# An attention and max-out kernel: attention in four runs of matmuls per group, loads, decoding and weight splits placed anew

## The chip, the cores and the metric

The kernel runs on one NeuronCore of a Trainium2 chip. The metric is the device time of one execution in microseconds (us), lower is better. The engines are TensorE (PE: matmuls; its weight loads are a row of their own, PEld), VectorE (DVE), ScalarE (ACT), GpSimd (POOL) and SyncE (SP, which issues nearly all DMAs).

## The reference

Attention with a sigmoid instead of a softmax feeds a layer that takes the largest of three products, and one more product.

```python
scores = scale * q @ k.T - log(S)          # batch 8, 12 heads, S = 448, head width 64
attn_out = sigmoid(scores) @ v
x = attn_out.transpose(0, 2, 1, 3).reshape(8 * 448, 12 * 64)     # 3584 x 768
h = maximum(maximum(x @ w1, x @ w2), x @ w3)                     # each weight 768 x 768
out = h @ w_out
```

## The kernel before

**Attention.** Heads are taken in pairs (one qk tile holds q and k of two heads, 64 partitions each) and two pairs make a group, so there are 24 groups, the loop over `n` at L394. Keys come in three chunks of 128 and a remainder of 64. `scores` (L325) multiplies one chunk for both heads of a pair side by side, in three fp32r terms made of high and low parts (`qk_split`, L317, on VectorE), and ends in one sigmoid of 2 x 448 columns on ScalarE. `last_scores` (L336) does the remainders of both pairs in plain F32, `weigh` (L348) multiplies a chunk's sigmoids by v in F32, `last_weigh` (L355) does so for the remainder. An F32 matmul stands in the trace as two records. A group's order on TensorE is: the first pair's scores, the second pair's weighing of the group before and its `last_weigh`, `last_scores`, the second pair's scores, the first pair's weighing. Scores go through three tiles `ps_s` of two PSUM banks each, weighing through two banks `ps_av`. `finish` (L373) copies these out on VectorE and stores them to `x_dram`.

Beside this, weights are decoded from 64-bit floats in blocks (`decoding`, L156; two steps on ScalarE, four on VectorE), combined on GpSimd (`w_combine`) and split into high and low parts (`w_split`, L151). From group 9 on, x blocks are loaded back and combined on GpSimd (`x_combine`).

Before the first group, 12 matmuls on zeros run (L388). TensorE's clock has two levels, 1.2 and 2.4 GHz.

**Layers.** Four stages (three weights and the output weight) times four pairs of batches make 16 visits (`n` at L507). A visit has three passes `q`, each of seven products of 2x2 blocks (`PRODUCTS`, L28) with nine fp32r matmuls of 448 columns (`product`, L446), so 16 x 3 x 7 x 9 = 3024 matmuls. A place is written (n, q, k). Before a product's operand can be used, ScalarE casts its high part (`x_hi`, L257) and VectorE subtracts (`x_lo`, L263). Tables fix the places: `his` and `los` for x, `ws` for weight splits, `w_loads` for weight loads and combinations, `decodes` for decoding. `put` (L515) adds a product's bank to what it needs on VectorE and, where a block is done, stores it. The turn into the last stage is at visit 12.

Everything runs in the order of the program on each engine (`pin`), SP's queue included: a load that waits for its buffer holds back what stands behind it.

Of the kernel before, what the change touches and what calls it, by code (L numbers as in the profile page):

```python
# [17 lines left out]
P = 128  # L18
D = 64
# [3 lines left out]

# [12 lines left out]
def attention_then_maxout(  # L40
# [8 lines left out]

# [29 lines left out]
    xs_p = pool(ctx, "xs", 1)  # L100
# [3 lines left out]


# [20 lines left out]


# [28 lines left out]
    def decoding(dec_p, todo, bufs, ahead, square_p):  # L156
# [35 lines left out]
        for k, (st, q, n) in enumerate(todo):  # L192
            while len(raws) < min(k + ahead, len(todo)):
                raws.append(load(*todo[len(raws)]))
            if k == 0:
                yield
# [13 lines left out]

    def x_block(r, src, p, row, th, k=None):

        name = f"b{row + 1}{th + 1}"
        if name not in r:
            r[name] = xs_p.tile([P, HALF, S], F32, name=f"xs_{name}")
        ks = slice(0, HALF) if k is None else slice(k, k + 1)
        t = (2 * p + th) * S
        pin(nc.sync.dma_start(out=r[name][:, ks], in_=src[row][:, ks, t : t + S]))

    def x_combine(r, names=TOKENS, ks=range(HALF)):  # L220

        for name in names:
            if name not in r:
                r[name] = (
                    r["b12"] if name == "t3" else xs_p.tile([P, HALF, S], F32, name=f"xs_{name}")
                )
# [13 lines left out]
    def t_store(r, p):  # L240
        for k, name in enumerate(TOKENS):
            pin(nc.sync.dma_start(out=t_dram[p][:, k], in_=r[name]))

    def x_load_all(p):
        r = {}
        for _, name, _ in PRODUCTS:
            if name in TOKENS:
                tile_name = "xs_b12" if name == "t3" else f"xs_{name}"
                r[name] = xs_p.tile([P, HALF, S], F32, name=tile_name)
# [18 lines left out]
    def attention(stack):  # L268

        dec_p = pool(stack, "dec", 2)
        sq_p = pool(stack, "sq", 2)
# [3 lines left out]
        a_p = pool(stack, "a", 8)  # L277
# [5 lines left out]
        background = decoding(dec_p, todo, 2, 3, sq_p)  # L283
        splits = []

# [10 lines left out]
        def load_qk(b, k):  # L296
            t = qk_p.tile([P, 2 * S], F32, name="qk")
            if b == k == 0:
# [11 lines left out]
        def sigmoid(ps):  # L310
            a = a_p.tile([P, 2, S], F32, name="a")
            pin(nc.scalar.activation(  # L312
                out=a, in_=ps[:, :, :S], func=AF.Sigmoid, bias=bias_s, scale=scale
            ))
            return a
# [9 lines left out]
        def scores(terms, c):  # L325
            ps = ps_s.tile([P, 2, 512], F32, name="ps_s")
            for n, (kt, qt) in enumerate(terms):
                for e in range(2):
                    r = slice(e * D, (e + 1) * D)
                    pin(nc.tensor.matmul(  # L330
                        ps[:, e, :S], kt[r, S + c * P : S + (c + 1) * P], qt[r, :S],
                        start=n == 0, stop=n == len(terms) - 1,
                    ))
            return sigmoid(ps)

        def last_scores(ts):  # L336
# [9 lines left out]
            return sigmoid(ps)  # L346

        def weigh(ps, vt, g, c, a):  # L348
            for e in range(2):
                pin(nc.tensor.matmul(  # L350
                    ps[e * D : (e + 1) * D, :S], vt[:, (g * C + c) * 2 + e], a[:, e],
                    start=c == 0, stop=False,
                ))

        def last_weigh(pss, vt, a):  # L355
            for g, ps in enumerate(pss):
                r = slice(g * D, (g + 1) * D)
                for e in range(2):
                    pin(nc.tensor.matmul(
                        ps[e * D : (e + 1) * D, :S], vt[r, 4 * C + e], a[r, e],  # L360
                        start=False, stop=True,
# [5 lines left out]
        def load(n):  # L367
            if n < len(fours):
                b, f = fours[n]
                ts = load_qk(b, 2 * f), load_qk(b, 2 * f + 1)  # L370
                loads[n] = ts, load_v(b, f)

        def finish(n, pss, pool=m_p, names=("m11", "m12")):  # L373
            b, f = fours[n]
            for g, ps in enumerate(pss):
# [7 lines left out]
        load(0)  # L383

# [3 lines left out]
        for n in range(12):  # L388
# [4 lines left out]
        terms = [(loads[0][0][0],) * 2]  # L393
        for n in range(len(fours) + 1):  # L394
            if n < len(fours):
                load(n + 1)
                ts, vt = loads.pop(n)
                first = [scores(terms, c) for c in range(C)]
                terms = qk_split(ts[1])
                if n == 0:  # L400
                    decode()
                for _ in range(2):
                    if splits:
                        w_split(*splits.pop(0), nc.vector.tensor_copy)
# [3 lines left out]
            if before:  # L408
                pvt, pss, second, last = before
                for c in range(C):  # L410
                    weigh(pss[1], pvt, 1, c, second[c])
                last_weigh(pss, pvt, last)
                if n == len(fours):
                    break
# [208 lines left out]
```

## Time and profile before

| | us |
|---|---|
| median of three runs | 884.75 |
| lowest, highest | 883.69, 893.62 |
| span of the profiled execution | 882.5 |
| TensorE busy in the span | 874.1 |

The span reaches from the first to the last instruction of the profiled execution; the run's time also holds what lies around it. TensorE's busy time counts from a matmul's start to its modelled end, and matmuls overlap, so the steps between starts tell more than the share. "x12" merges twelve records of one kind; "[1.21 <-DMA qk<-qk]" is idle time ahead of a group and what ended it. In the windows, the columns are the stretch, its length, and for PE, PEld, DVE, ACT and POOL the busy time with the number of instructions, then the granted clock, the DMA engines' busy share and GB/s.

### The profile page before, as it was taken

To read this page: it belongs to the slowest core of one execution; us is meant where nothing else is said; L and a number is where in the kernel's file an instruction comes from. 1 tells how busy PE (TensorE), PEld (TensorE's weight loads), DVE (VectorE), ACT (ScalarE), POOL (GpSimd) and SP (SyncE) were. 2 spreads that over 40 slices of the span, in tenths; PEclk is the share of its full clock that TensorE was granted. 3 is DMA by queue.
4 is the path that set the end of the run, shared out by engine and by line. 5 is a ranking of instruction groups with operands and counts; after the bars stand their busy time and mean duration, and the time that the engine had idled before them with its cause. 6 is when DMAs were issued, how large, how long until landed. Compare 5 with 4: busy or idle time off the path is not lost. (4 is left out here: it accounts for less than half of the span.)

```text
span 882.5 us, 12993 instructions
## 1 busy us (share of the span) xinstructions
PE 874.1 (99%) x4866; PEld 696.1 (79%) x4866; DVE 621.3 (70%) x875; ACT 392.9 (45%) x499; POOL 183.2 (21%) x148
## 2 busy tenths in 40 slices
PE   8999999999999999999999999999999999999998
PEld 4544455444459999999999999999999998899997
DVE  3677568766866948678696888878778596736442
ACT  5777767776672413342353343235334253423320
POOL 0100022023102563502100020210001543760600
PEclk9999999999999999999999999999999999999999
DMA  6667666786647455414745642484563426162412
GB/s 225 208 227 240 226 236 224 243 279 228 214 158 275 174 217 165 174 50 141 292 159 207 241 147 70 148 298 170 182 263 114 150 77 222 65 209 94 169 72 83
DMA packets 74350, 161.87 MB, mean 183 GB/s; under 512 B 6960, under 2 KB 53808, under 8 KB 74288
## 3 DMA queue, kind: packets, MB, share of 16 engines
q1 hardware_dynamic: 74208, 160.82, 52.0%
q8 instruction: 38, 0.62, 0.3%
q10 hardware_dynamic: 80, 0.23, 0.1%
q14 instruction: 24, 0.20, 0.1%
HBM read 109.90 MB, written 51.12 MB: 182 GB/s over the span
## 5 line engine op out<-in xcount | busy, mean ns | idle before, releaser
L312 ACT ACTIVATE a<-ps_s,bias_s 128x896 f32<-128x896 f32 x168 | 156.4, 1007 | 78.6 <-PE ps_s L342 59.4
L451 PE MATMUL ps_y<-xhi_t,wlo_s 128*128 128x448 f32 x432 | 158.1, 366 | 0.1
L451 PE MATMUL ps_y<-xhi_t,whi_s 128*128 128x448 f32 x432 | 158.0, 366 | 0.0
L451 PE MATMUL ps_y<-xlo_t,whi_s 128*128 128x448 f32 x432 | 157.9, 366 | 0.0
L350 PE MATMUL ps_av<-a,v 128*64 128x448 f32 x576 | 118.6, 548 | 0.0
L451 PE MATMUL ps_y<-xhi_b,wlo_a 128*128 128x448 f32 x288 | 105.4, 366 | 0.0
L451 PE MATMUL ps_y<-xlo_b,whi_a 128*128 128x448 f32 x288 | 105.3, 366 | 0.0
L451 PE MATMUL ps_y<-xhi_b,whi_a 128*128 128x448 f32 x288 | 105.3, 366 | 0.0
L141 POOL TENSOR_TENSOR ws_s<-ws_a,ws_a 128x384 f32<-128x384 f32 x12 | 14.3, 1194 | 412.9 <-DMA ws_a<-w_dram 315.8
L549 ACT COPY p<-ps_y 128x448 f32<-128x448 f32 x48 | 25.5, 531 | 156.4 <-PE ps_y L451 156.4
L451 PEld LDWEIGHTS ps_y<-xhi_t,wlo_s 128*128 128x128 f32 x432 | 81.3, 188 | 6.8 <-ACT xhi_b L260 0.5
L451 PEld LDWEIGHTS ps_y<-xhi_t,whi_s 128*128 128x128 f32 x432 | 81.3, 188 | 6.3
L451 PEld LDWEIGHTS ps_y<-xlo_t,whi_s 128*128 128x128 f32 x432 | 81.3, 188 | 6.2
L350 PEld LDWEIGHTS ps_av<-a,v 128*64 128x64 f32 x576 | 37.2, 136 | 59.4 <-issue 57.9
L523 DVE TENSOR_TENSOR m<-ps_y,u 128x448 f32<-128x448 f32 x72 | 44.7, 621 | 55.9 <-PE ps_y L451 55.9
L229 POOL TENSOR_TENSOR xs_t<-xs_b,xs_t 128x448 f32<-128x448 f32 x48 | 64.2, 1363 | 37.0 <-DMA xs_b<-x_dram 36.0
L264 DVE TENSOR_TENSOR xlo_t<-xs_t,xhi_t 128x1344 fp32r<-128x1344 f32 x42 | 68.4, 1628 | 3.0 <-ACT xhi_t L260 3.0
L521 ACT COPY m<-ps_y 128x448 f32<-128x448 f32 x24 | 12.8, 533 | 125.8 <-PE ps_y L451 122.2
L552 DVE TENSOR_TENSOR u<-ps_y,p 128x448 f32<-128x448 f32 x48 | 29.9, 622 | 53.6 <-PE ps_y L451 52.5
L264 DVE TENSOR_TENSOR xlo_b<-xs_b,xhi_b 128x1344 fp32r<-128x1344 f32 x42 | 66.5, 1584 | 0.0
L260 ACT CAST xhi_t<-xs_t 128x1344 fp32r<-128x1344 f32 x42 | 55.5, 1322 | 17.7 <-PE ps_y L451 9.0
L175 ACT ACTIVATE c<-wraw 128x384 f32<-128x384 f32 x48 | 27.0, 563 | 75.4 <-DVE m L529 44.9
(68 smaller groups left out, 1636.1 us busy)
## 6 DMA issues: line engine op xcount, KB each, us to landing
qk<-qk SPq DMA_DIRECT2D x47, 448.0 KB, 5.6
xs_b<-x_dram SPq DMA_DIRECT2D x30, 672.0 KB, 7.0
wraw<-w SPq DMA_DIRECT2D x36, 384.0 KB, 4.9
xs_t<-t_dram SPq DMA_DIRECT2D x18, 672.0 KB, 8.0
v<-v SPq DMA_DIRECT2D x24, 448.0 KB, 3.8
h_dram<-m SPq DMA_DIRECT2D x48, 224.0 KB, 1.9
xs_b<-h_dram SPq DMA_DIRECT2D x16, 672.0 KB, 6.5
outT<-m SPq DMA_DIRECT2D x48, 224.0 KB, 1.9
```

The source lines that it names most:

```text
L141: pin(nc.gpsimd.tensor_tensor(out=r[name], in0=r[in0], in1=r[in1], op=op))
L175: pin(nc.scalar.activation(out=square, in_=high.bitcast(F32), func=AF.Square))
L229: pin(nc.gpsimd.tensor_tensor(out=r[name][:, k], in0=r[in0][:, k], in1=r[in1][:, k], op=ALU.subtract))
L260: pin(nc.scalar.copy(out=hi, in_=r[name]))
L264: pin(nc.vector.tensor_tensor(out=lo, in0=x, in1=hi.bitcast(F32), op=ALU.subtract))
L312: pin(nc.scalar.activation(out=a, in_=ps[:, :, :S], func=AF.Sigmoid, bias=bias_s, scale=scale))
L350: pin(nc.tensor.matmul(ps[e * D : (e + 1) * D, :S], vt[:, (g * C + c) * 2 + e], a[:, e], start=c == 0, stop=False,))
L451: pin(nc.tensor.matmul(ps[:, :S], wt[:, k * P : (k + 1) * P], xt[:, k], start=first and n == 0, stop=n == len(terms) - 1, skip_group_check ...
L521: pin(nc.scalar.copy(out=m[name], in_=y))
L523: pin(nc.vector.tensor_tensor(out=m[name], in0=y, in1=add, op=ALU.add))
L549: pin(nc.scalar.copy(out=p1, in_=ps[0][:, :S]))
L552: pin(nc.vector.tensor_tensor(out=u2, in0=ps[1][:, :S], in1=p1, op=ALU.add))
```

## The change

Attention's order in a group becomes: `last_scores`, all six score chunks, then for the group before all six weighings and `last_weigh`. The third chunk of the first pair writes its scores to the `ps_av` banks as two tiles, with one sigmoid for each; the other chunks keep `ps_s`. In group 23 `last_weigh` comes before the weighings. qk tiles are loaded two groups ahead and v in its own group; the first two qk tiles come in halves over two queues. Both pairs' splits for the next group are made in the group before. The loads of raw weight blocks (`fetch`) and their decoding are separate steps, with fewer buffers; one block's decoding moves from attention to place (1, 0, 6), and the x operand t4 is combined and stored after attention. 18 matmuls run on zeros instead of 12. One matmul, at (0, 1, 0), takes 478 columns instead of 448. In the turn to the last stage the weight splits of the first set move from visit 11's second pass to its first, those of the second set from visit 12 partly to visit 11, the third set's from k = 4 to 6 to k = 2 to 4 of the second pass, and with them the weight loads; the x load of visit 12 moves from k = 6 to k = 4. The very last block is added and stored in two halves, the second one over ScalarE's queue.

```diff
-        sq_p = pool(stack, "sq", 2)
+        sq_p = pool(stack, "sq", 1)
-        a_p = pool(stack, "a", 8)
+        a_p = pool(stack, "a", 9)
...
-        background = decoding(dec_p, todo, 2, 3, sq_p)
+        todo.insert(19, todo.pop(15))
+        todo.pop()
+        background = decoding(dec_p, todo, 1, 2, sq_p)
...
-            if b == k == 0:
+            if b == 0 and k < 2:
                 pin(nc.scalar.dma_start(out=t[D:], in_=qk[b, k, D:]))
                 pin(nc.sync.dma_start(out=t[:D], in_=qk[b, k, :D]))
...
+        def sigmoid(banks, **kw):
+            a = a_p.tile([P, 2, S], F32, name="last" if kw else "a", **kw)
+            parts = (
+                [(a[:, e], ps[:, :S]) for e, ps in enumerate(banks)]
+                if type(banks) is list else [(a, banks[:, :, :S])]
+            )
+            for out, ps in parts:
+                pin(nc.scalar.activation(
+                    out=out, in_=ps, func=AF.Sigmoid, bias=bias_s, scale=scale
+                ))
             return a
...
+        def accumulators():
+            return [ps_av.tile([P, 512], F32, name=f"ps_av{g}") for g in range(2)]
...
+        def weigh(banks, vt, chunks, ahead):
+            for g, ps in enumerate(banks):
+                for c, a in enumerate(chunks[g]):
+                    for e in range(2):
+                        pin(nc.tensor.matmul(
+                            ps[e * D : (e + 1) * D, :S], vt[:, (g * C + c) * 2 + e], a[:, e],
+                            start=c == 0 and not ahead, stop=c == C - 1 and ahead,
+                        ))
...
         load(0)
+        load(1)
...
-        for n in range(12):
+        for n in range(18):
...
             if n < len(fours):
-                load(n + 1)
-                ts, vt = loads.pop(n)
-                first = [scores(terms, c) for c in range(C)]
-                terms = qk_split(ts[1])
+                ts = loads.pop(n)
+                if n != 1:
+                    fetch()
+                if n:
+                    last = last_scores(ts)
+                    load(n + 2)
+                    vt = load_v(*fours[n])
+                    for _ in range(2):
+                        if splits:
+                            w_split(*splits.pop(0), nc.vector.tensor_copy)
+                first = [scores(terms[0], c, accumulators() if c == C - 1 else None)
+                         for c in range(C)]
                 if n == 0:
+                    terms = None, qk_split(ts[1])
+                    last = last_scores(ts)
+                    vt = load_v(*fours[n])
+                    load(n + 2)
+                ahead = loads.get(n + 1)
+                after = [qk_split(ahead[0]) if ahead else None]
+                if n:
                     decode()
+                second = [scores(terms[1], c) for c in range(C)]
+                after.append(qk_split(ahead[1]) if ahead else None)
+                terms = after
...
-                x_combine(xs, ((), ("t1",), ("t2", "t3"), ("t4",))[block], (k,))
+                x_combine(xs, ((), ("t1",), ("t2", "t3"), ())[block], (k,))
...
+            if before:
+                pvt, chunks, rest = before
+                banks = accumulators()
+                if n == len(fours) - 1:
+                    last_weigh(banks, pvt, rest, True)
+                    weigh(banks, pvt, chunks, True)
+                else:
+                    weigh(banks, pvt, chunks, False)
+                    last_weigh(banks, pvt, rest, False)
+                if n < len(fours):
+                    finish(n - 1, banks)
+            before = vt, (first, second), last
...
+            moving, cols = xt[:, k], S
+            if wide and n == 0:
+                cols = S + 30
+                moving = xt[:].rearrange("p a s -> p (a s)")[:, :cols]
...
             else:
-                when = [[(n - 1, 1, 4 + k // 3) for k in range(7)],
-                        [(n, 0, 1)] * 2 + [(n, 0, 4)] * 2 + [(n, 0, 5)] * 2 + [(n, 0, 6)],
-                        [(n, 1, 4 + k // 3) for k in range(7)]]
+                when = [[(n - 1, 0, k) for k in (1, 1, 4, 4, 4, 5, 6)],
+                        [(n - 1, 2, 5)] + [(n - 1, 2, 6)] * 2 + [(n, 0, 4)] * 4,
+                        [(n, 1, 2 + k // 3) for k in range(7)]]
...
-    decodes = [
+    decodes = [(1, 0, 6)] + [
...
-    todo = [(st, q, n) for st in (2, 3) for q in range(3) for n in range(4)]
+    todo = [(1, 2, 3)] + [(st, q, n) for st in (2, 3) for q in range(3) for n in range(4)]
...
-    for _, name, _ in PRODUCTS[1:4]:
+    x_combine(xs, ("t4",))
+    for _, name, _ in PRODUCTS[1:5]:
         x_lo(*x_hi(name, xs))
...
+                    elif (n, q, name) == (done - 1, 2, "12"):
+                        row, t = q * P, (2 * p + 1) * S
+                        for r, dma in ((slice(0, S // 2), nc.sync), (slice(S // 2, S), nc.scalar)):
+                            pin(nc.vector.tensor_tensor(
+                                out=m[name][:, r], in0=y[:, r], in1=add[:, r], op=ALU.add
+                            ))
+                            pin(dma.dma_start(
+                                out=outT[row : row + P, t + r.start : t + r.stop],
+                                in_=m[name][:, r],
+                            ))
+                        return
...
-                product(ps[bank], w_ops[q][wname], x_ops[xname], first)
+                product(ps[bank], w_ops[q][wname], x_ops[xname], first, here == (0, 1, 0))
...
-                if here == (n, 0, 6 if (n, 0, 6) in w_loads else 4) and nst in (0, LAST):
+                if here == (n, 0, 4) and nst in (0, LAST):
                     xs = x_load(x_dram if nst == 0 else h_dram, np_)
```

## Rows read from the trace of the kernel before

**Rows 1.** The page, busy time, share of the span, instructions by engine

```profile
PE 874.1 (99%) x4866; PEld 696.1 (79%) x4866; DVE 621.3 (70%) x875; ACT 392.9 (45%) x499; POOL 183.2 (21%) x148
```

**Rows 2.** Timeline of TensorE (PE) at the start: start, duration, line, operation

```profile
1.05 2.93 PE L391 MATMUL ps_s<-idle 64*128 64x128 f32 x24 [1.05 <-DVE bias_s L87]
5.19 4.74 PE L330 MATMUL ps_s<-qk 64*128 64x448 f32 x12 [1.21 <-DMA qk<-qk]
9.86 0.98 PE L342 MATMUL ps_s<-qk 64*64 64x448 f32 x8
```

**Rows 3.** Timeline of VectorE (DVE), start and first groups

```profile
7.33 0.63 DVE L321 CAST hi<-qk 128x896 fp32r<-128x896 f32 x1 [6.33 <-DMA qk<-qk]
7.99 1.09 DVE L322 TENSOR_TENSOR lo<-qk,hi 128x896 fp32r<-128x896 f32 x1
...
20.65 1.16 DVE L378 COPY m<-ps_av 128x448 f32<-128x448 f32 x2 [2.29 <-PE ps_av L359]
```

**Rows 4.** Timeline of TensorE over one attention group

```profile
20.43 0.93 PE L342 MATMUL ps_s<-qk 64*64 64x448 f32 x8
21.30 0.47 PE L330 MATMUL ps_s<-hi 64*128 64x448 f32 x2
21.60 0.36 PE L330 MATMUL ps_s<-lo,hi 64*128 64x448 f32 x2
...
22.62 0.43 PE L330 MATMUL ps_s<-hi 64*128 64x448 f32 x2
22.89 0.37 PE L330 MATMUL ps_s<-lo,hi 64*128 64x448 f32 x2
23.09 0.37 PE L330 MATMUL ps_s<-hi,lo 64*128 64x448 f32 x2
23.39 2.48 PE L350 MATMUL ps_av<-a,v 128*64 128x448 f32 x12
25.80 0.47 PE L330 MATMUL ps_s<-hi 64*128 64x448 f32 x2
...
31.02 0.93 PE L342 MATMUL ps_s<-qk 64*64 64x448 f32 x8
```

**Rows 5.** Timeline of TensorE at the end of attention

```profile
256.30 4.73 PE L350 MATMUL ps_av<-a,v 128*64 128x448 f32 x24
260.96 0.98 PE L359 MATMUL ps_av<-a,v 64*64 64x448 f32 x8
261.87 0.47 PE L451 MATMUL ps_y<-xhi_b,wlo_a 128*128 128x448 f32 x1
```

**Rows 6.** Timeline of ScalarE (ACT) in the same group as rows 4

```profile
21.52 3.70 ACT L312 ACTIVATE a<-ps_s,bias_s 128x896 f32<-128x896 f32 x4 [2.60 <-PE ps_s L342]
25.09 0.58 ACT L175 ACTIVATE c<-wraw 128x384 f32<-128x384 f32 x1
```

**Rows 7.** Busy time of each engine in stretches of the layers

```profile
400.00:500.00 100.00, 100.00 (x495) 92.82 (x494) 79.35 (x120) 36.28 (x52) 8.11 (x8) 1.00 0.54 194
600.00:700.00 100.00, 100.00 (x495) 92.80 (x495) 77.16 (x104) 37.27 (x46) 9.89 (x9) 1.00 0.53 192
700.00:800.00 100.00, 97.65 (x477) 88.87 (x476) 71.23 (x85) 38.10 (x50) 52.83 (x40) 1.00 0.37 129
```

**Rows 8.** Waits of TensorE by line and releaser, total, times, longest

```profile
PE ps_y L451 <- DVE m L523: 2.1, 1, 2.1
```

**Rows 9.** Timeline of GpSimd (POOL) in the turn

```profile
747.25 4.45 POOL L229 TENSOR_TENSOR xs_t<-xs_b,xs_b 128x448 f32<-128x448 f32 x3 [3.48 <-DMA xs_b<-h_dram]
```

**Rows 10.** Timeline of VectorE in the turn

```profile
758.05 2.26 DVE L264 TENSOR_TENSOR xlo_t<-xs_t,xhi_t 128x1344 fp32r<-128x1344 f32 x1 [2.98 <-ACT xhi_t L260]
```

**Rows 11.** Last addition on VectorE, and stores by kind

```profile
878.78 0.62 DVE L523 TENSOR_TENSOR m<-ps_y,u 128x448 f32<-128x448 f32 x1 [1.21 <-PE ps_y L451]
...
outT<-m SPq DMA_DIRECT2D x48, 224.0 KB, 1.9
...
w_dram<-wb SPq DMA_DIRECT2D x36, 192.0 KB, 1.9
```

More of the change, by code (lines that the diff above doesn't have):

```diff
@@ L209, in attention_then_maxout, with xs_tile @@
     TOKENS = tuple(SUMS)
+    def xs_tile(name):
+        return xs_p[name == "t4"].tile([P, HALF, S], F32, name=f"xs_{name}")
     def x_block(r, src, p, row, th, k=None):
@@ L214, in x_block @@
         if name not in r:
-            r[name] = xs_p.tile([P, HALF, S], F32, name=f"xs_{name}")
+            r[name] = xs_tile(name)
         ks = slice(0, HALF) if k is None else slice(k, k + 1)
@@ L223, in x_combine @@
             if name not in r:
-                r[name] = (
-                    r["b12"] if name == "t3" else xs_p.tile([P, HALF, S], F32, name=f"xs_{name}")
-                )
+                r[name] = r["b12"] if name == "t3" else xs_tile(name)
             in0, in1 = SUMS[name]
@@ L323, in qk_split, with scores @@
             return (hi, hi), (hi, lo), (lo, hi)
-        def scores(terms, c):
-            ps = ps_s.tile([P, 2, 512], F32, name="ps_s")
+        def accumulators():
+            return [ps_av.tile([P, 512], F32, name=f"ps_av{g}") for g in range(2)]
+        def scores(terms, c, banks=None):
+            if banks is None:
+                banks = ps_s.tile([P, 2, 512], F32, name="ps_s")
+            bank = banks if type(banks) is list else [banks[:, e] for e in range(2)]
             for n, (kt, qt) in enumerate(terms):
@@ L345, in last_scores, with last_weigh @@
                     ))
[L346 to L356, printed above, removed]
+            return sigmoid(ps, bufs=2)
+        def weigh(banks, vt, chunks, ahead):
[6 more added lines that the diff above has]
+                        ))
+        def last_weigh(banks, vt, a, ahead):
+            for g, ps in enumerate(banks):
                 r = slice(g * D, (g + 1) * D)
@@ L360, in last_weigh @@
                         ps[e * D : (e + 1) * D, :S], vt[r, 4 * C + e], a[r, e],
-                        start=False, stop=True,
+                        start=ahead, stop=not ahead,
                     ))
@@ L407, in attention @@
                     x_lo(*x_hi(name, xs))
[L408 to L414, printed above, removed]
-                finish(n - 1, pss)
-            last = last_scores(ts)
-            second = [scores(terms, c) for c in range(C)]
-            if n + 1 < len(fours):
-                terms = qk_split(loads[n + 1][0][0])
-            decode()
             part = n - 9
@@ L426, in attention @@
                 x_block(xs, x_dram, 0, row, th, k)
-                x_combine(xs, ((), ("t1",), ("t2", "t3"), ("t4",))[block], (k,))
+                x_combine(xs, ((), ("t1",), ("t2", "t3"), ())[block], (k,))
             if n == len(fours) - 1:
-                t_store(xs, 0)
-            pss = [ps_av.tile([P, 512], F32, name=f"ps_av{g}") for g in range(2)]
-            for c in range(C):
-                weigh(pss[0], vt, 0, c, first[c])
-            before = vt, pss, second, last
+                t_store(xs, 0, TOKENS[:3])
+            if before:
[10 more added lines that the diff above has]
+            before = vt, (first, second), last
         assert not splits
-        return xs, lambda *to: finish(len(fours) - 1, pss, *to)
+        return xs, lambda *to: finish(len(fours) - 1, banks, *to)
     with ExitStack() as stack:
         xs, finish = attention(stack)
+    xs_p.append(pool(ctx, "xs2", 1, reuse_waits="tile"))
     xo_p.append(pool(ctx, "xo2", 1, reuse_waits="tile"))
@@ L444, in attention_then_maxout, with product @@
     ps_y = pool(ctx, "ps_y", 2, space=PSUM, reuse_waits="tile")
-    def product(ps, w, x, first):
+    def product(ps, w, x, first, wide):
         (w_hi, w_lo), (x_hi, x_lo) = w, x
```

45 lines of the change are left out of this document (20 added, 25 removed).

## The prediction

> **What bounds it now.** I read the busy shares, then TensorE's timeline, then the engines beside it. TensorE is busy 99% of the span [rows 1], so an edit counts only where it shortens TensorE's own sequence or a gap in it. The sequence has four parts.
>
> *Start.* Zeros run from 1.05, end near 4.0, then TensorE idles 1.21 us for the first qk tile. The first scores take 5.19 to 9.86, 4.67 us for 12 records [rows 2]. The same number of F32 records takes 2.41 us later (23.39 to 25.80) [rows 4]. So these run at half pace, the 1.2 GHz level of the two, although the granted clock column reads 1.00 there.
>
> *Attention.* One group takes 31.02 - 20.43 = 10.59 us with no gap, but with seams. A pair of score matmuls (64 rows x 128 columns, two side by side) steps every 0.20 us. The first pair after another shape takes 0.30 (21.30 to 21.60), and so does the last one before another shape (23.09 to 23.39). One pair takes 0.27 (22.62 to 22.89) [rows 4]: it waits for the bank that the sigmoid begun at 21.52 reads for 1.01 us [rows 6]. Twelve weighing records between scores take 2.41; the 24 in a row at the end of attention take 260.96 - 256.30 = 4.66, 0.16 less than twice 2.41 [rows 4, 5].
>
> *Layers.* 495 matmuls per 100 us, 0.202 us each, without a gap [rows 7].
>
> *The turn into the last stage.* Between 700 and 800 us only 477 matmuls stand [rows 7]: 18 x 0.202 = 3.6 us lost. The longest single loss is 2.1 us behind a VectorE addition, L523 [rows 8].
>
> **The change, part by part.**
>
> *Runs of matmuls.* Before, a group went scores, weigh, last_weigh and last_scores (both 64x64, one shape), scores, weigh: five changes of shape. After: last_scores, six score chunks, six weighings, last_weigh: three. Two weigh blocks become one (-0.16), two score runs become one: one slow first pair (-0.10) and one slow exit (-0.10) go. That is 0.36 us per group; groups 1 to 23 have both seams, 23 x 0.36 = 8.3. No matmul is added.
>
> *The waits this adds.* Seven chunks now follow each other 0.61 us apart (3 x 0.20), while ScalarE takes 0.90 each (four in 3.70, the last 1.01) [rows 6]. In time from last_scores: its sigmoid starts at 1.09 (21.52 - 20.43), chunk 1's at 1.09 + 2 x 0.90 = 2.89, ending 3.90. The last chunk reuses that buffer at 0.87 + 0.30 + 14 x 0.202 = 4.00; with a release of 0.16 (sigmoid ends 22.53, TensorE goes on near 22.69) it goes at 4.06. So 0.06 of wait with the weighings queued behind it, what the old order also pays (0.27 - 0.20). Chunk 2 of the first half goes to the weighing banks, and its sigmoid is cut in two so that weighing needs only the first half. That half starts at 3.79 and ends near 4.4, plus release 4.6; weighing comes at 4.8. Two halves instead of one whole cost ScalarE one more start; bounds 0 and 1.01 (a whole one), I take 0.2, in which it has cover: 7 x 0.90 + 0.2 + two decode steps of 0.58 [rows 6] is 7.7 of 10.2 us.
>
> Those banks are free again only when the copies of `finish` are through: 1.16 us, starting 0.22 after the group's end [rows 3, 4], thus ending 1.4 into the next group; chunk 2 comes at 2.2. Cover 0.8 us. Before, nothing but weighing used those banks. VectorE is busy for 70% of the span [rows 1], some 7 us of a group, so the copies are seldom late. I take the wait as 0, at most 0.3 a group.
>
> *Loads and decoding.* `fetch` goes to the head of the group and loads a raw block one group (10 us) before it is decoded; qk tiles are loaded two groups ahead, v one group before its weighing. On SP the copies' stores now stand ahead of the next group's fetch and loads, which therefore go out some 1.4 us into a group; behind a load that waits for its buffer stand v, the weight store and the x block. The first need is the split, near 3 us into the following group. Cost 0. Without that cover each us late would be a us.
>
> *Start.* 18 zeros instead of 12 at 2.93 per 24 records [rows 2] end at about 5.4, 0.2 after the tile has landed. The clock had risen by 9.86, at most 4.7 us after unbroken work began at 5.19; unbroken work now begins at 1.05, so by 5.7. The first scores then take about 2.5, to 8.0, and last_scores 0.9, to 8.9. The next scores need the second tile, landed at 7.33 and split by 7.99 + 1.09 = 9.08 [rows 3]; they start at 9.15 instead of 10.77: 1.6 gained. Bounds: -0.2 (clock as before) and 2.0 (tile earlier).
>
> *A queue that speaks against.* That tile comes in two halves on two queues. The Trainium skill (DMA: Bandwidth & Descriptors, Issuing engines are not separate DMA queues) says that such queues share the same engines, so that only issue time is saved. By it the tile lands at 7.3 still and the gain is 1.6; were the rate doubled it would be 2.0.
>
> *Moved to the layers.* The t4 subtractions (POOL), one block's decode (visit 1) and a fourth operand split go behind attention. t4 is needed at product 5 and b21 at product 4, 36 x 0.202 = 7.3 us after the layers' start; a cast and a subtraction, each at most the 2.26 that the latter takes with POOL beside it [rows 10], fit. Cost 0, at most 1 us. VectorE has 21% idle in the layers at 400 to 500 us [rows 7] for the decode.
>
> *Turn into the last stage.* POOL combines x from 747.25 on, after the third weight set [rows 9]; xlo waits 2.98 us for its cast, ends 760.3 [rows 10], and L523 queues behind it; TensorE waits for that. The change issues these loads two products earlier (18 x 0.202 = 3.6 us) and moves the first splits away from VectorE's full stretch. On SP the weight loads still stand ahead of x and wait for the splits before them, so the shift is 3 to 3.6. What is late next is t4 in visit 13, shifted as well. Of 3.6 us lost I take 3.0 back; bounds 0 and 3.6.
>
> *Wide matmul.* 30 more of 448 columns, once: at most 30/448 x 0.202 = 0.014 us.
>
> *Last block.* Addition 0.62, then a transfer of 1.9 [rows 11]. In halves the second addition ends up to 0.3 later than the one did, and its transfer is half. Bounds -0.4 (a landing time that does not shrink, and the issue on ScalarE) and +0.9 (1.9 halved). 192 KB land in 1.9 us as 224 KB do [rows 11], so it is near the first; I take 0.1.
>
> Sum: 8.3 + 1.6 + 3.0 + 0.1 = 13.0. The profiled span is 882.5; around it lie some 2.25 us to the median 884.75, which no edit touches. 884.75 - 13 = 871.75, so **872 us**, 1.4% faster. The ends of the terms: attention 8.3 - 23 x 0.3 = 1.4 to 9.7 (also the old wait gone), start -0.2 to 2.0, turn 0 to 3.6, tail -0.4 to 0.9, layers' start -1 to 0: 885 to 868.5.
>
> **Rivals.**
>
> *A. New waits eat the attention gain.* Copies late on VectorE, or a sigmoid behind a decode that waits for its raw block: 0.3 us a group is 7 us, which leaves 879. For: the banks' cover is only 0.8 us and VectorE is 70% busy [rows 1]. Against: everything else has 2 us and more.
>
> *B. The layers' pace falls after the new phase (other side).* Weight loads are busy 92.8 of 100 us [rows 7], so each matmul follows its load closely and the pace hangs on how the two interlock. At 0.207 instead of 0.202, from visit 0's second third on, 2961 x 0.005 = 15 us are lost: 887, slower than before. It decides from 13/2961 = 4.4 ns. For: one of three runs took 893.62, 9 us more, which 3 ns per layer matmul would explain; this profile cannot show it. Against: 400 to 500 and 600 to 700 us count the same 495, and the score runs step at 0.20 after each seam.
>
> *C. The pace rises.* The weighing steps, 4.66/12 = 0.39 for two streams of 448 columns by their ratio to 0.202, give 0.194 a stream [rows 5]. At that the layers lose 2961 x 0.008 = 24 us: 848. The wide matmul would have to bring this about; against it stands the constant pace. [...]
>
> *D. The turn keeps its stall or the clock rises as late as before.* 874 to 877, inside the forecast's own range.
>
> **Chances.** Forecast with D 0.73 (own range 867 to 877), A 0.12 (877 to 884), B 0.06 (885 to 895), C 0.09 (below 865). Eight in ten: 867 to 880, which leaves out C, most of B and part of A. About 2% is what a measurement of this kernel tells from no change; 2% faster is 867. Faster: C and the forecast's lowest edge, 0.09 + 0.04 = 0.13. Slower than 902: a part of B, 0.02. Within 2%: 0.85.
>
> **What would show it.** The group period, last_scores to last_scores, near 10.2 instead of 10.59; 24 weighing records in a row in 4.66 in each group; no 0.30 step between the two halves of the scores; layers starting near 252 instead of 261.87 [rows 5]. First scores done by 8.2. In the turn no wait of TensorE over 0.5 us. The layers at 495 matmuls per 100 us. It is wrong if the period stays over 10.4 (A), if the layers' count per 100 us moves by more than five (B, C), or if the first scores still take over 4 us.

## The result, and the profile after

The changed kernel takes 870.5 us (median of six runs, 869.89 to 874.24) against 884.01 for the kernel before beside it (six runs, 881.87 to 893.62): a ratio of 0.9848, 95% interval 0.9814 to 0.9882, 13.5 us. The forecast was 872. The profiled execution of after took 873.77, span 872.0; one more has 872.4, and the spans of the four others are 868.1 to 869.0. Against the 882.5 of before it gains 10.5, and where these come from is not quite what the prediction says.

Page of after, busy time and instructions by engine:

```profile
PE 867.2 (99%) x4878; PEld 700.9 (80%) x4878; DVE 617.8 (71%) x876; ACT 395.5 (45%) x523; POOL 181.0 (21%) x148
```

It looks like [rows 1]: the shares tell nothing of a change of 1.5%. The steps, the times from one matmul's start to the next one's, do.

**Start.** Timeline of TensorE of after:

```profile
1.05 4.21 PE L375 MATMUL ps_s<-idle 64*128 64x128 f32 x36 [1.05 <-DVE bias_s L60]
5.14 1.89 PE L312 MATMUL ps_s<-qk 64*128 64x448 f32 x8
6.86 0.92 PE L312 MATMUL ps_av<-qk 64*128 64x448 f32 x4
7.71 0.98 PE L324 MATMUL ps_s<-qk 64*64 64x448 f32 x8
...
9.26 0.47 PE L312 MATMUL ps_s<-lo,hi 64*128 64x448 f32 x2 [0.18 <-DVE lo L299]
...
11.15 0.98 PE L324 MATMUL ps_s<-qk 64*64 64x448 f32 x8
```

VectorE of after at the split of the second qk tile, and TensorE of before where the first group's scores end:

```profile
7.45 0.63 DVE L298 CAST hi<-qk 128x896 fp32r<-128x896 f32 x1 [6.45 <-DMA qk<-qk]
```

```profile
12.80 2.48 PE L350 MATMUL ps_av<-a,v 128*64 128x448 f32 x12
```

The zeros now reach the first scores without a gap. The trace's record of the clock begins at full speed at 5.41 here and at 9.69 in before; ahead of that record the clock column reads 1.00 too, and the steps alone tell the pace. So the first scores go at half pace only for the first 0.3 us and are through at 7.71 instead of 9.86 [rows 2]; then 0.18 us pass in waiting for the second tile's low part. That tile's split starts at 7.45, in before at 7.33 [rows 3]: the halves over two queues didn't bring it earlier. The first group's scores end at 11.15 instead of 12.80, 1.65 earlier.

**A group.** TensorE between two `last_scores`, then the sigmoids of that stretch (ScalarE) and the copies of `finish` (VectorE):

```profile
93.12 0.93 PE L324 MATMUL ps_s<-qk 64*64 64x448 f32 x8
93.98 0.47 PE L312 MATMUL ps_s<-hi 64*128 64x448 f32 x2
94.29 0.36 PE L312 MATMUL ps_s<-lo,hi 64*128 64x448 f32 x2
...
95.31 0.36 PE L312 MATMUL ps_av<-hi 64*128 64x448 f32 x2
...
97.83 4.73 PE L334 MATMUL ps_av<-a,v 128*64 128x448 f32 x24
102.49 0.98 PE L343 MATMUL ps_av<-last,v 64*64 64x448 f32 x8
103.29 0.93 PE L324 MATMUL ps_s<-qk 64*64 64x448 f32 x8
```

```profile
94.15 1.01 ACT L289 ACTIVATE last<-ps_s,bias_s 128x896 f32<-128x896 f32 x1 [2.67 <-PE ps_s L324]
...
96.84 1.17 ACT L289 ACTIVATE a<-ps_av,bias_s 128x448 f32<-128x448 f32 x2
```

```profile
93.34 1.16 DVE L361 COPY m<-ps_av 128x448 f32<-128x448 f32 x2 [1.75 <-PE ps_av L343]
```

The period is 103.29 - 93.12 = 10.17 us instead of 10.59 [rows 4]. The 24 weighing records take 4.66 (97.83 to 102.49), and the only long first step of a score pair (0.31) is from 93.98 to 94.29. The copies end at 94.50, and the third chunk writes to their banks at 95.31: 0.8 us of cover (the time that the banks are free ahead of their need). The layers start at 251.35 instead of 261.87 [rows 5]:

```profile
251.35 0.47 PE L451 MATMUL ps_y<-xhi_b,wlo_a 128*128 128x448 f32 x1
```

**Layers.** Windows of after, columns as in [rows 7]:

```profile
400.00:500.00 100.00, 100.00 (x496) 92.76 (x495) 75.13 (x114) 33.87 (x46) 4.00 (x4) 1.00 0.61 223
700.00:800.00 100.00, 100.00 (x486) 90.85 (x485) 68.40 (x78) 40.40 (x50) 43.48 (x33) 1.00 0.37 130
```

No gap is left between 700 and 800 us, where before lost 18 steps; and yet only 486 matmuls stand there, not 495. The granted clock reads 1.00 in both. Timeline of TensorE of after, just ahead:

```profile
683.81 0.37 PE L451 MATMUL ps_y<-xhi_t,whi_a 128*128 128x448 f32 x1
684.01 0.37 PE L451 MATMUL ps_y<-xhi_b,wlo_s 128*128 128x448 f32 x1
684.28 0.47 PE L451 MATMUL ps_y<-xlo_b,whi_s 128*128 128x448 f32 x1
684.59 0.37 PE L451 MATMUL ps_y<-xhi_b,whi_s 128*128 128x448 f32 x1
684.79 0.37 PE L451 MATMUL ps_y<-xhi_b,wlo_s 128*128 128x448 f32 x1
```

One step takes 0.27 instead of 0.20: a wait of 0.07 us for `xlo_b` at (11, 0, 6). The step behind it takes 0.31, so the wait costs 0.17 in all. From there on nearly every step is 0.206 or 0.207, and so it stays to the end. There are two paces: 202.7 ns per matmul (the **short step**; a pattern of 199 to 207 that repeats after five) and 206.7 (the **long step**, nearly all alike). From the first matmul of a visit to that of the next, 189 matmuls, 38.30 or 39.06 us pass. Why the operand was late, VectorE in the same stretch:

```profile
679.21 0.55 DVE L123 TENSOR_TENSOR wlo_a<-ws_a,whi_a 128x384 fp32r<-128x384 f32 x1
679.67 0.55 DVE L123 TENSOR_TENSOR wlo_s<-ws_s,whi_s 128x384 fp32r<-128x384 f32 x1
...
682.68 1.55 DVE L233 TENSOR_TENSOR xlo_b<-xs_b,xhi_b 128x1344 fp32r<-128x1344 f32 x1
```

Two splits that the change put into the first pass of visit 11 stand ahead of the subtraction, which ends at 684.23; VectorE has no idle time between. They are not enough by themselves: in the traces of experiments 1, 2, 4 and 11 they stand at the same place, and the same subtraction ends 0.40, 0.27, 0.59 and 1.01 us ahead of its matmul.

**Tail.** The last additions on VectorE, then the stores of kind `outT` by queue with KB and median landing time:

```profile
868.51 0.69 DVE L522 TENSOR_TENSOR m<-ps_y,u 128x224 f32<-128x224 f32 x2 [1.23 <-PE ps_y L451]
```

```profile
outT<-m SPq DMA_DIRECT2D x47, 224.0 KB, 1.9
outT<-m SPq DMA_DIRECT2D x1, 112.0 KB, 1.7
outT<-m ACTq DMA_DIRECT2D x1, 112.0 KB, 1.7
```

From the start of the last matmul to the end 3.88 us instead of 4.10.

Span before to span after: start 1.65, attention 8.9, waits of the turn 3.6, tail 0.2 are gained (14.3); the long step from visit 11 on costs 3.56, the same in the first pass of visit 0 another 0.25. That makes 10.5. Only this execution was traced; that the other one near 874 has the same cause is likely by its time and not shown.

### The profile page after: what moved, and what is told of

It is laid out like the page before. It is cut to its first block, busy times and chain, and to the rows that moved or that the text cites. A ratio compares the mean times of both kernels' runs of the same rounds, so it can differ in the third digit from the quotient of the medians.

```text
span 872.0 us, 12969 instructions
## 1 busy us (share of the span) xinstructions
PE 867.2 (99%) x4878; PEld 700.9 (80%) x4878; DVE 617.8 (71%) x876; ACT 395.5 (45%) x523; POOL 181.0 (21%) x148
## 4 chain that ended last, share of the span: by engine, by line
PE 99%; DMA 1%; DVE 0%; SPq 0%; DVEq 0%; issue 0%
PE ps_y L451 71%; PE ps_av L334 13%; PE ps_s L312 9%; PE ps_av L343 3%; PE ps_s L324 2%; PE ps_av L312 2%; DMA qk<-qk 1%; DVE lo L299 0%; DVE hi L298 0%; SPq L272 0%; DVE m L522 0%; DVEq L630 0%; DVEq L298 0%
## 5 line engine op out<-in xcount | busy, mean ns | idle before, releaser
L289 ACT ACTIVATE a<-ps_s,bias_s 128x896 f32<-128x896 f32 x120 | 112.9, 1006 | 4.0 <-PE ps_s L312 2.9
L334 PE MATMUL ps_av<-a,v 128*64 128x448 f32 x576 | 113.3, 543 | 0.0
L334 PEld LDWEIGHTS ps_av<-a,v 128*64 128x64 f32 x576 | 39.4, 137 | 63.5 <-issue 56.9
```

The lines of the kernel that those rows point to most:

```text
L289: pin(nc.scalar.activation(out=out, in_=ps, func=AF.Sigmoid, bias=bias_s, scale=scale))
L334: pin(nc.tensor.matmul(ps[e * D : (e + 1) * D, :S], vt[:, (g * C + c) * 2 + e], a[:, e], start=c == 0 and not ahead, stop=c == C - 1 and a ...
```

## The experiments

Experiments 1 to 5 and 11 start from the kernel after, 6 to 10 from experiment 5, and 12 from the kernel before. In the expectations "fast" and "slow" pace are the short and the long step. Ratios stand against the kernel before, run beside it on the same chip. From experiment 6 on a table `WIDER` gives the columns by which the first matmul of a product is widened beyond 448, by its place; it takes the place of the one wide matmul at (0, 1, 0).

**1. The wide matmul narrow again.**

```diff
-            if wide and n == 0:
+            if False and wide and n == 0:
```

> The changed kernel with the one wide matmul back at 448 columns, nothing else. Theory (two paces: in the profile of the changed kernel the layers step at 206.6 ns before the wide matmul and after a wait at place (11, 0, 6), and at 202.6 ns between; the wide matmul moves the stream from the slow to the fast pace): the layers start at 206.7 ns and stay there until some wait resets them, so up to 2960 x 4 ns = 11.8 us more, 880 to 882 us if nothing resets them. Rival (the pace comes from elsewhere, the wide matmul does nothing): 870 to 874 us as the changed kernel, with 202.6 ns in visits 1 to 10.

870.19 us (four runs), ratio 0.9842 [0.9826, 0.9859], span 868.0. Its layers went at the short step from the first matmul, and no wait came:

```profile
700.00:800.00 100.00, 100.00 (x495) 92.69 (x494) 70.06 (x79) 40.71 (x50) 42.58 (x32) 1.00 0.39 133
```

So an execution can do without the wide matmul, and the expected 880 or so was missed: all four runs lie at 869.8 to 870.75. Of what the wide matmul does where the layers begin at the long step, this says nothing.

**2. One seam back.** The first pair's weighing goes between the two pairs' scores again, as before, and the third chunk goes to a `ps_s` tile again, with one whole sigmoid.

```diff
+                split_run = before and n < len(fours) - 1
+                if split_run:
+                    banks = accumulators()
+                    weigh(banks, before[0], before[1], False, (0,))
                 second = [scores(terms[1], c) for c in range(C)]
```

> The changed kernel with the first pair's weighing put between the two halves of the scores again in groups 1 to 22; the third chunk then goes to a ps_s tile with one whole sigmoid. Theory (the gain in attention is the price of two changes of matmul shape per group): the group's period goes from 10.17 to 10.53 us (0.16 + 0.10 + 0.10), 22 x 0.36 = 7.9 us more, 878 to 879. Rival (the gain came from the banks and from splits and loads made earlier, so that TensorE no longer waits): period 10.17 to 10.25, 870 to 872.

877.89 us, ratio 0.9928 [0.9913, 0.9942]; layers start at 259.03. TensorE in a group:

```profile
98.80 2.48 PE L336 MATMUL ps_av<-a,v 128*64 128x448 f32 x12
101.21 0.47 PE L312 MATMUL ps_s<-hi 64*128 64x448 f32 x2
101.52 0.36 PE L312 MATMUL ps_s<-lo,hi 64*128 64x448 f32 x2
```

The step of 0.31 after the weighing is back (101.21 to 101.52), and the period is 10.51 instead of 10.17. By the steps of a group the two changes of shape cost 0.345 us, with no other wait over 0.01; the layers start 7.7 us later. The prediction had 0.36 per group. The Trainium skill (TensorEngine Tiling (Array Packing), Key Properties) says that a change of tiling mode drains TensorE; the 0.345 us fit this, though the trace shows the longer steps and not a drain as such.

**3. The turn as before.** Weight splits and x load of the last turn at their old places.

```diff
-                when = [[(n - 1, 0, k) for k in (1, 1, 4, 4, 4, 5, 6)],
-                        [(n - 1, 2, 5)] + [(n - 1, 2, 6)] * 2 + [(n, 0, 4)] * 4,
-                        [(n, 1, 2 + k // 3) for k in range(7)]]
+                when = [[(n - 1, 1, 4 + k // 3) for k in range(7)],
+                        [(n, 0, 1)] * 2 + [(n, 0, 4)] * 2 + [(n, 0, 5)] * 2 + [(n, 0, 6)],
+                        [(n, 1, 4 + k // 3) for k in range(7)]]
...
-                if here == (n, 0, 4) and nst in (0, LAST):
+                if here == (n, 0, 6 if (n, 0, 6) in w_loads else 4) and nst in (0, LAST):
```

> The changed kernel with the places of weight splits, weight loads and the x load around the turn to the last stage as before. Theory of the prediction: the waits of about 3.6 us in visits 11 to 13 come back, so the turn costs 3 to 3.7 us more than without waits. Theory of two paces adds: the wait at (11, 0, 6) goes, visit 11 keeps 202.6 ns, and whichever pace the later waits leave behind decides the rest: 873.5 with the fast one, 876.5 with the slow one. Rival (the new places gained nothing because the moved splits only shift the wait): 870 to 871.

876.74 us, ratio 0.9908 [0.989, 0.9926]. Waits of TensorE by releaser, then windows behind the longest:

```profile
PE ps_y L451 <- DVE m L531: 2.1, 1, 2.1
PE ps_y L451 <- DVE xlo_t L233: 0.9, 1, 0.9
```

```profile
752.00:756.00 4.00, 4.00 (x14) 3.59 (x13) 2.89 (x2) 3.93 (x4) 4.00 (x3) 0.57 0.26 95
756.00:800.00 44.00, 44.00 (x215) 39.97 (x214) 24.49 (x28) 15.22 (x16) 13.77 (x13) 1.00 0.39 139
```

The waits of [rows 8] are back, 3.65 us by the steps. The rest is new: after the longest one (2.2 by the steps) the granted clock fell (0.57 in this stretch, the 1.2 GHz level in most of it; 1.5 us lost), and then the long step ran for the last three visits (2.3 us). The kernel before lost neither after the same wait, which is why the prediction's 3.6 was not the whole price. Waits 3.65 (less the 0.17 that after has too), clock 1.5 and long step 2.3 are the 7.3 by which the span of 875.7 exceeds 868.4, the span of after without the 3.56 of its last visits. Of the four runs (873.86 to 877.44) the shortest is where the waits alone would put it; it wasn't traced.

**4. Start and tail as before.**

```diff
-        for n in range(18):
+        for n in range(12):
```

with the last block added and stored whole.

> The changed kernel with 12 matmuls on zeros instead of 18 and the last block in one piece; the two lie in stretches of the trace that do not touch. Theory: the first scores run at half pace again and end near 9.8 instead of 7.7; the layers start 1.6 to 2.0 us later than 251.35; after the last matmul 0.2 us more pass than the 3.88 of the changed kernel. Rival for the start (the clock rises as early because the loads end TensorE's idling sooner): first scores done by 8.2, layers start as in the changed kernel.

873.93 us (two runs, 872.15 and 875.71; the first is the traced one), ratio 0.9882 [0.9856, 0.9909]. TensorE:

```profile
5.11 3.36 PE L312 MATMUL ps_s<-qk 64*128 64x448 f32 x8 [1.12 <-DMA qk<-qk]
...
9.89 1.23 PE L324 MATMUL ps_s<-qk 64*64 64x448 f32 x8
```

The first scores end 2.18 later than in after, the layers start 2.1 later, the tail is 0.23 longer. The second run's 3.6 us more are not explained.

**5. The two early splits two places later.**

```diff
-                when = [[(n - 1, 0, k) for k in (1, 1, 4, 4, 4, 5, 6)],
+                when = [[(n - 1, 0, k) for k in (3, 3, 4, 4, 4, 5, 6)],
```

> The changed kernel with the first two weight splits of visit 11 at k = 3 instead of k = 1, behind VectorE's xlo that TensorE waited for at (11, 0, 6). Theory (that wait of 0.07 us left the slow pace behind): no wait of TensorE in the turn, 202.7 ns to the end whatever pace the layers start with, span 868.2 to 868.5, time 870. Rival (the slow pace comes late in the layers by itself, heat or clock): 206.7 ns again from some place on, span up to 872.

870.14 us (four runs), ratio 0.9831 [0.9803, 0.9859]. No wait of 0.07 came, and no late long step:

```profile
700.00:800.00 100.00, 100.00 (x495) 92.72 (x495) 70.30 (x80) 40.70 (x50) 44.21 (x34) 1.00 0.37 132
```

The subtraction ends 0.60 us ahead of its matmul. In experiment 4, with the two splits at their early place, it was 0.59 ahead:

```profile
683.92 1.54 DVE L233 TENSOR_TENSOR xlo_b<-xs_b,xhi_b 128x1344 fp32r<-128x1344 f32 x1
```

```profile
686.06 0.36 PE L451 MATMUL ps_y<-xlo_b,whi_s 128*128 128x448 f32 x1
```

So this experiment doesn't show that the later place is what removed the wait. None of the twelve runs with it (here, 8 and 10) lies near 874, against two of six of after; but none of the four of experiment 1 does either, with the early place.

Its layers began at 206.6 ns, and with the wide matmul at (0, 1, 0) went over to 202.7. The same happened in every profile with that matmul whose layers began long (after, 3, 5, 6, 10, 11). Whether waits and the widening cause this or only stand beside it is what the next ones ask.

**6. A wait in every visit.** VectorE copies 64 columns of a finished bank, and one added matmul reads them; widening in every other visit. The waits came out at 0.6 to 3.8 us.

```diff
+WIDER = {(0, 2, 0): 30, (2, 2, 0): 30, (4, 2, 0): 30, (6, 2, 0): 30, (8, 2, 0): 30, (10, 2, 0): 30, (12, 2, 0): 30, (14, 2, 0): 30, (0, 1, 0): 30}
...
+                if n and (q, k) == (1, 4):
+                    z = c_p.tile([P, 64], F32R, name="z", bufs=1)
+                    pin(nc.vector.tensor_copy(out=z, in_=ps[bank][:, :64]))
+                    scratch = ps_av.tile([P, 512], F32, name="ps_av0")
+                    pin(nc.tensor.matmul(scratch[:, :64], w_ops[q][wname][0][:, :P], z, start=True, stop=True))
```

> The kernel of e5_late_splits with a wait made at place (v, 1, 4) of each visit from 1 on (VectorE copies 64 columns of the product just done, one added matmul reads them, some 0.6 us of wait each) and the wide matmul at (v, 2, 0) of the even visits alone. Theory of two paces: after each wait the stream runs at either 202.7 or 206.7 ns and keeps it until the next wait; in even visits it is 202.7 from pass 2 on always, in odd visits a slow pace, where the wait left one, lasts through pass 2 and into the next visit. At least 2 of 15 waits leave the slow pace. Rival (paces come and go with time): slow stretches that begin or end away from waits and wide matmuls.

905.7 us (one run); most of what lies above 870 is the added waits. Windows of 34 us, each from behind the place of the widening to the next wait:

```profile
400.00:434.00 34.00, 34.00 (x170) 31.53 (x169) 22.46 (x42) 10.55 (x24) 3.97 (x4) 1.00 0.62 227
647.00:681.00 34.00, 34.00 (x166) 30.89 (x165) 25.65 (x35) 13.17 (x15) 1.05 (x2) 1.00 0.57 213
...
849.00:883.00 34.00, 34.00 (x170) 31.46 (x168) 18.30 (x21) 11.71 (x12) 3.24 (x3) 1.00 0.17 62
```

The second follows the wait of visit 9, which has no widening: 166 matmuls instead of 170. The last lies behind the widening of visit 14, whose wait had left the long step. Of the 15 waits 4 left the long step (visits 4, 9, 13, 14), 11 the short one. A long step that met no widening lasted until the next wait; the widening ended it in visits 4 and 14. In visit 0, however, a widening turned the short step into the long one. After the two longest waits, 3.8 us each, the granted clock fell to half (395.0 to 398.4 and 562.3 to 565.7).

**7. Other widths.**

```diff
+WIDER = {(1, 2, 0): 10, (2, 2, 0): 20, (3, 2, 0): 44, (4, 2, 0): 64, (5, 2, 0): 10, (6, 2, 0): 20, (7, 2, 0): 44, (8, 2, 0): 64, (9, 2, 0): 10, (10, 2, 0): 20, (11, 2, 0): 44, (12, 2, 0): 64, (13, 2, 0): 10, (14, 2, 0): 20, (15, 2, 0): 44}
```

> As e6_waits_wide, but the first matmul of (v, 2, 0) is widened in every visit from 1 on, by 10, 20, 44, 64 columns in turn. Theory: the widening works by shifting the stream against something with a fixed beat, so some of these widths end a slow pace and some don't, and none ends a fast one. Rival (any disturbance of the stream draws the pace anew, as a wait does): some visits go from fast to slow at the widened matmul.

918.59 us (one run). TensorE at a widening by 10 (458 columns) in visit 9:

```profile
654.28 0.37 PE L453 MATMUL ps_y<-xhi_b,wlo_s 128*128 128x448 f32 x1
...
655.50 0.37 PE L453 MATMUL ps_y<-xhi_b,wlo_a 128*128 128x458 f32 x1
...
661.08 0.37 PE L453 MATMUL ps_y<-xhi_t,wlo_s 128*128 128x448 f32 x1
```

Six steps ahead of it (654.28 to 655.50) take 1.22 us, the 27 behind it (655.50 to 661.08) 5.58: from 0.203 to 0.207 with no wait between them. Where the layers came from the long step, plus 10 left it as it was (visits 1, 5, 13), plus 20 (14) and plus 44 (11) ended it. Where they came from the short step, plus 10 and plus 20 went over to the long one (9; 2, 10), plus 44 and plus 64 did so at some places (15; 4) and not at others (7; 8, 12). In visits 3 and 6 the clock was at its lower level until two or three steps ahead of the widening, so which step they came from can't be read. The expectation was that none would end a short step. A widening thus is no remedy that can be put anywhere: it can end a long step, and can spoil a short one. Several of these cases are single ones.

**8. The widening earlier.** Experiment 5 with the widening at the layers' second product.

```diff
+WIDER = {(0, 0, 1): 30}
```

> The kernel of e5_late_splits with the wide matmul at (0, 0, 1), the tenth matmul of the layers, instead of (0, 1, 0). Theory: as e5, and where the layers start slow only 10 instead of 64 matmuls are slow: 0.2 us less, 869.8 to 870. Rival: the wide matmul needs its place at (0, 1, 0), slow layers: over 875.

870.0 us (869.97 to 870.63), ratio 0.9832 [0.9808, 0.9855]. Its layers began at the short step, so the earlier place shows nothing. The time is within the uncertainty of after's median.

**9. Four widenings by 10.** They stand in the first pass; the widening by 30 is taken out.

```diff
+WIDER = {(0, 0, 1): 10, (0, 0, 2): 10, (0, 0, 3): 10, (0, 0, 5): 10}
...
-                product(ps[bank], w_ops[q][wname], x_ops[xname], first, here == (0, 1, 0))
+                product(ps[bank], w_ops[q][wname], x_ops[xname], first, WIDER.get(here, 0))
```

> The kernel of e5_late_splits without the wide matmul at (0, 1, 0), and with the first matmul of products 1, 2, 3 and 5 of the layers widened by 10 columns, which in e7_waits_widths left a slow pace slow (3 of 3) and made a fast one slow (1 of 1). Theory: the layers fall into 206.7 ns in their first pass and, with no wait behind, stay there: 2960 x 4 ns = 11.8 us more than the 870.1 of e5_late_splits, 881 to 882. Rival (the slow pace passes by itself): 870 to 873.

882.12 us (ten runs, 881.73 to 882.71), ratio 0.9968 [0.9948, 0.9988]. Every visit takes 39.06 us (the first 39.13), to the end. The traced execution had the long step from the third matmul on, ahead of the first widening: here the widenings by 10 left a long step as it was, as in experiment 7. That they can also begin it is seen in experiment 12.

**10. The same with one matmul of 478 columns behind it.**

```diff
-WIDER = {(0, 0, 1): 10, (0, 0, 2): 10, (0, 0, 3): 10, (0, 0, 5): 10}
+WIDER = {(0, 0, 1): 10, (0, 0, 2): 10, (0, 0, 3): 10, (0, 0, 5): 10, (0, 1, 0): 30}
```

> The kernel of e9_start_slow with the wide matmul (478 columns) at (0, 1, 0) again. Theory: it ends the slow pace as in all seven cases seen, 202.7 ns from pass 1 on, 870.1 to 870.5, 11.6 us below e9_start_slow. Rival (the wide matmul only draws anew): in some runs 881.

870.02 us (869.9 to 870.14), ratio 0.9834 [0.9808, 0.9861]. The same window in 9, then in 10:

```profile
400.00:500.00 100.00, 100.00 (x486) 90.84 (x485) 75.19 (x114) 34.67 (x49) 3.98 (x4) 1.00 0.57 209
```

```profile
400.00:500.00 100.00, 100.00 (x495) 92.76 (x494) 74.99 (x114) 33.88 (x46) 3.98 (x4) 1.00 0.61 222
```

The two kernels differ in 30 columns of one matmul and in 12.1 us by their medians, 11.8 by the two spans (880.2 and 868.4): the 2961 matmuls behind the first pass times 4.0 ns. In both traces the layers began at the long step, and in 10 it ended at the wide matmul. The granted clock is 1.00 in both, and the engines beside TensorE do nearly the same work. Of the cases seen before that the expectation counts, the traces hold six: after, 3, 5 and three places of 6.

**11. The copies of `finish` made twice.**

```diff
-                pin(nc.vector.tensor_copy(out=o, in_=ps[:, :S]))
+                for _ in range(2):
+                    pin(nc.vector.tensor_copy(out=o, in_=ps[:, :S]))
```

> The changed kernel with each copy of the weighing banks in finish made twice, 1.16 us more on VectorE ahead of the banks' release in each group. Theory of the prediction (those banks have 0.8 us of cover before the third chunk's scores need them): the copies end near 2.5 into the group and the chunk waits 0.4 to 0.6 us, plus 0.1 for a slow first pair; the period goes from 10.17 to between 10.6 and 10.9, 10 to 16 us more in all. Rival (the banks are free long before, cover over 1.2 us): period 10.17 to 10.25, time as the changed kernel.

886.6 us, ratio 1.0016 [0.9983, 1.0048]; period 10.89. TensorE:

```profile
101.57 0.44 PE L312 MATMUL ps_av<-hi 64*128 64x448 f32 x1 [0.29 <-DVE m L362]
```

The third chunk now waits for the copies that free its banks. Another 1.16 us per group is more than the cover of 0.8, and takes away the whole gain of the change. So the mechanism of rival A is real; with the copies made once it doesn't act.

**12. The widenings of 9 in the kernel before.** `product` gets the same change for it.

```diff
+WIDER = {(0, 0, 1): 10, (0, 0, 2): 10, (0, 0, 3): 10, (0, 0, 5): 10}
```

> The kernel before, with the first matmul of products 1, 2, 3 and 5 of its layers widened by 10 columns as in e9_start_slow. Theory (the kernel before's runs of 893 to 895 are executions whose layers fell into the slow pace at their start): the layers step at 206.7 ns from their first pass to the first wait, at place (12, 0, 5), matmul 2313, which is 9.3 us, and then by what the waits leave: 892 to 897. Rival (those runs have another cause, a late clock or a late load): the layers step at 206.7 too, but the time is not that of those runs; or the kernel before has no slow pace, 884.

891.87 us (eight runs, 890.4 to 893.31) against 884.18, ratio 1.0083 [1.0056, 1.011]. Windows:

```profile
400.00:500.00 100.00, 100.00 (x486) 90.81 (x485) 77.60 (x118) 36.33 (x52) 8.71 (x8) 1.00 0.52 185
780.00:860.00 80.00, 80.00 (x395) 73.89 (x394) 41.34 (x47) 24.49 (x26) 26.78 (x24) 1.00 0.41 147
```

The layers began at the short step, and at the second widening, their 19th matmul, went over to the long one. It lasts until the wait of [rows 8] in visit 12, and behind it 395 matmuls in 80 us are short steps. The traced execution (890.66) is below the 892 expected; in it the clock rose early, and the layers started 1.9 us earlier than in before:

```profile
5.20 2.53 PE L332 MATMUL ps_s<-qk 64*128 64x448 f32 x12 [1.22 <-DMA qk<-qk]
```

The unchanged kernel's scattered runs have about this size: over all experiments 5 of 48 took 890.33 to 894.58, the others 881.8 to 888.3. None of the five was traced, so whether this is their cause stays open.

## Why the prediction was right, and where it was not

The median came out 1.5 us below the forecast, inside its range. By its steps:

- **Runs of matmuls: right.** 8.3 forecast, 8.9 measured. Experiment 2 shows the two seams to be worth 0.345 per group, for a forecast of 0.36. The wait of 0.06 for the last chunk was forecast to stay and is gone in the steady state: the sigmoid of `last_scores` starts 1.03 after them (93.12 to 94.15), not 1.09. Against this stand 0.6 us that groups 1 and 2 take longer than the later ones; ScalarE runs there without a break.
- **Cover of the `ps_av` banks: right.** 0.8 us, and the wait was taken as 0; experiment 11 shows where it ends.
- **Loads and decoding, the work moved to the layers: right.** No wait of TensorE stands there.
- **Start: right in size, 1.65 for 1.6, but not as sure as written.** With the old 12 zeros the trace's record of the clock's rise is at 9.69 in before, 10.45 in experiment 4 and 4.42 in experiment 12, whose first scores were through at 7.65. So an execution with the old start can have the gain too. With 18 zeros it rose at 4.52 to 6.54 in all eleven traces: the late rise was not seen there, though the forecast's "by 5.7" was passed in three of them.
- **Turn: the waits right, the rest missed.** Waits of 3.75 us are down to 0.17 (3.0 forecast, 3.6 gained). The change put two splits ahead of `xlo_b` in visit 11, and the prediction costed the moved splits at nothing. In the profiled execution a wait of 0.07 us came there, which by itself would be nothing; in four other traces with the same places none came.
- **Rival B, "the pace falls": came true in part, in the profiled execution.** The forecast named 0.207 as its pace. What failed is the argument against it: that two windows of one trace count 495 was read as a constant of the machine. It is one of two paces, and behind a wait either can follow. Experiments 9 and 10 show the price, 12 us over all layers; here the long step held five visits and cost 3.56. That B was given a chance of 0.06 and the time still came out near the forecast is in part luck: the same wait in visit 1 would have cost some 11 us (an estimate: 0.76 us in each of 15 visits).
- **Wide matmul: the term that was mis-sized.** 0.014 us was forecast, for its columns. It is worth up to 12 us where the layers begin at the long step (experiment 10), and nothing where they begin at the short one (experiment 1). Of the twelve traces whose attention and layers' start are those of after or nearly so (after, 1 to 11), seven began long; over executions of after itself the share wasn't measured, so what the wide matmul is worth to it on average isn't known.
- **Tail: right.** 0.2 for 0.1. A half block lands in 1.7 us, a whole one in 1.9. The Trainium skill (DMA: Bandwidth & Descriptors, Anatomy of one DMA) gives a transfer a large fixed part, fitted on another path than these queues; the two landing times agree in so far as half the bytes saved only 0.2 us.
- **Rivals A, C and D:** not so. No stretch of the layers went below the short step in any experiment.

What stays open is why a wait leaves one pace or the other, why widenings of the same width differ by their place, and how often an execution of after meets the wait in visit 11.

## What to carry to other kernels

In a gap-free stream of matmuls, read the step between starts over a whole stretch and compare several executions before taking it as a constant: 4 ns per matmul are invisible in busy shares and in the granted clock, and over all layers were worth 12 us here, nearly as much as the whole change. A wait of 0.07 us can cost far more than itself in what comes after it (3.56 us here), so small waits in a long uniform stream are worth removing even where their own time is nothing. Where matmuls of different shapes alternate, put those of one shape together, and check which buffer then becomes free last and by how much.

## What the hardware showed that was not expected

- The layers' streams of weight load and fp32r matmul of 448 columns had two stable paces at a granted clock of 1.00, 202.7 and 206.7 ns. A wait may change one into the other (4 of 15 in experiment 6 left the long one), and so may one matmul of other width: 478 columns ended a long pace in after and in experiments 3, 5, 6, 10 and 11; 458 columns began one with no wait at all (visit 9 of experiment 7, and experiment 12).
- The granted clock fell after a wait of 2.2 us in experiment 3 (0.57 over 752 to 756 us) and after two of 3.8 us in experiment 6; the same wait of 2.2 us in the kernel before left it alone.
- With the same 12 zeros the clock rose at 4.42, 9.69 and 10.45 us in three traces.
